# An attention-and-adapters kernel on one core: from a planned order of the engines to one written out as a table

## The chip, the cores and the metric

One core of one Trainium2 chip runs the kernel. The metric is the device time of one execution in microseconds; the median of several runs counts. The engines are PE (matmul), DVE (VectorE), ACT (ScalarE), POOL (GpSimd) and SP (SyncE, which here only issues DMAs). Each works off its own queue in the order in which the program issues instructions.

## The reference

Two stages follow each other. The first is a linear attention with a decaying state, for 4 batches, 8 heads, 768 steps and head size 48:

```
state = alpha[t, :, None] * state + outer(k[t], v[t])
y[t]  = q[t] @ state
```

The second takes y as x, 3072 rows of 384, through a mixture of 8 adapters of rank 16, of which each row uses the best 2:

```
logits = x @ w_gate                      # 384 -> 8
w = softmax over the best two logits
out = x + sum over those two e of w[e] * (x @ A[e]) @ B[e]
```

## The kernel before

The work is cut into 24 units: one batch and one chunk of 128 steps, all 8 heads at once. Units 0 to 11 are the chunks of batches 0 and 1 by turns, units 12 to 23 those of batches 2 and 3; unit u hands its state on to unit u + 2. For each unit:

- `ln` (ACT) takes logarithms of alpha, for two units in one instruction from unit 2 on; `cum` (PE) adds them up along the chunk; `exp` (ACT, two instructions) makes the decay factors for k and q.
- `kg` (POOL) multiplies k and q with them; it is called the product below. `vb` (POOL) casts v. `tr` (PE) transposes the product, `kq` (ACT) copies the transposes out of PSUM, `at` (PE) makes the scores, `msk` (DVE) masks them: the mask product.
- `st` (DVE) scales the state, `kv` (PE) adds to it, `av` (PE) makes the unit's output, `ysb` (ACT) copies it out: the output copy. `xb` (POOL, even units) casts it, `xt` (PE) transposes it, `xs` (ACT) copies that out.

Units are then taken together in gate groups: three units each, the last two groups being [21, 22] and [23]. For a group `z` (PE) makes x @ [A, w_gate]; `gm` is the maximum, `df` the difference to it, `ge` the choice of the best two, `gx` (ACT) the exponential, `wu` its product with the choice, `dn` the sum, `w` the reciprocal and the multiplication with it, `zw` the weighted x @ A (all DVE but `gx`). `zt` (PE) and `zs` (ACT) turn it, and for each unit `dl` (PE) multiplies with B and `o` (DVE) adds the result to the output; a store on SP follows.

What sets the order: a planner at the top of the file, `_plan`, `_arrivals`, `_ops` and `_order`. It knows a length for each instruction, an arrival time for each load and a priority for each kind of step, places all steps in time, and the program issues them in that order. Loads come in pieces of two units (384 KB) on two rings: SP issues those of k and q mostly, ACT those of alpha and v, ACT's standing among its other instructions. Loads of SP wait for the ACT instruction that was issued last before them, so that both rings keep pace:

```
    def pump(now):
        while loaded[0] < len(plan[0]):
            item = plan[0][loaded[0]]
            if arr["due", item] > now or not set(_readers(item)) <= did:
                return
            load_next(0)
```

A load is due 6 us ahead of the time at which the planner expects its transfer to begin. Each of alpha, k with q, and v has six buffers of two units. Stores begin when all loads have been issued. PSUM has two banks for the scores, two for the states, and four that all other results share (`SLOTS`, `M_t`). `KEEP` says how many buffers a step's result has: logarithms 2 (of two units each), `exp` 4, products 4, `am` 3.

Of the kernel before, what the change touches and what calls it, by code (L numbers as in the profile page):

```python
# [93 lines left out]
def _readers(item):

    _, x, u, n = item
    for p in range(u - 2 * NS, u - 2 * NS + n):
        if p >= 0 and x != "w":
            if x == "a":
                yield "ln", next(us[0] for us in LNS if p in us)  # L100
            else:
                yield dict(k="kg", q="kg", v="vb")[x], p


def _arrivals(plan):
    arr, now = {}, 2.6
    at = [0, 0]
    left = [0., 0.]

    def start(r):  # L110
        if at[r] < len(plan[r]):
            x = plan[r][at[r]]
            left[r] = (.1, .1, .02, .2)[x[2]] if x[1] == "w" else .197 * x[3]
            arr["due", x] = now - LEAD
        else:
            left[r] = None

    start(0), start(1)
    while left != [None, None]:
        rate = .205 if None in left else RATE / 2  # L120
        step = min(x / rate for x in left if x is not None)
        now += step
        for r in range(2):
            if left[r] is not None:
                left[r] -= step * rate
                if left[r] < 1e-9:
                    _, x, u, n = plan[r][at[r]]
                    for j in range(n):
                        arr[x, u + j] = now + .4
                    at[r] += 1  # L130
                    start(r)
    return arr


def _ops(arr):
    ops = {}

    def add(name, eng, length, deps, war=(), alloc=None, frees=None):
        ops[name] = (eng, length, list(deps), list(war), alloc, frees)

    gof = {u: g for g, us in enumerate(GROUPS) for u in us}
    lof = {u: us for us in LNS for u in us}
    prev = []
    for i, item in enumerate(_plan()[1]):
# [130 lines left out]
def kernel(  # L275
# [66 lines left out]
    def load_next(r):  # L342
# [10 lines left out]
        if r == 0:  # L353
            behind(dma)
# [331 lines left out]
```

## Time and profile before

| what | value |
|---|---|
| median of 3 runs | 105.65 us (105.19 to 106.39) |
| profiled execution | 105.82 us |
| its span, first to last instruction | 104.1 us |
| busy: PE, DVE, ACT, POOL | 73.4, 69.3, 66.9, 61.2 us |
| instructions of PE, DVE, ACT, POOL | 1088, 169, 152, 70 |
| read from and written to memory | 19.28 MB, 4.72 MB |

Busy time is the time in which an engine worked on an instruction; waiting and issuing DMAs do not count. The profile is of one execution, and its times are microseconds from the first instruction. A released wait is put down to what came last by the profile.

### The profile page before, as it was taken

Reading aid. Unit: us, or ns where it says so; the run is one execution under the profiler, and the core shown is the slowest. Engines: PE = TensorE matmul, PEld = TensorE weight load, DVE = VectorE, ACT = ScalarE, POOL = GpSimd, SP = SyncE. Lnnn points to the kernel's source line nnn. Section 1 sums busy time; section 2 is a strip of 40 time slices with the busy share of each in tenths; the row PEclk is TensorE's granted clock in tenths of the full one; section 3 lists DMA queues with packets and bytes.
Section 4 is the critical chain, followed back from the end, with each engine's and each line's share of the span. In section 5 each row is a group of like instructions: output and inputs, shape, how many; then the busy total and the mean of one; then the engine's idle time right before and its main releaser. Section 6 shows DMA issues by size and latency. Waiting matters only on the chain.

```text
span 104.1 us, 2882 instructions
## 1 busy us (share of the span) xinstructions
PE 73.4 (70%) x1088; PEld 55.9 (54%) x1088; DVE 69.3 (67%) x169; ACT 66.9 (64%) x152; POOL 61.2 (59%) x70
## 2 busy tenths in 40 slices
PE   0020668679796499299798799748998899985450
PEld 0010555458574477177586667546787777854110
DVE  4000035414746799997758898798889899988980
ACT  4024327967379578169897896957979994953200
POOL 5006551791972972964949969498395979610000
PEclk9999999999999999958999999999999999999955
DMA  2999999999999999969999999999999999306173
GB/s 42 258 259 260 260 261 242 259 259 219 254 254 218 259 209 247 264 133 259 254 222 260 252 250 251 260 260 227 233 253 258 346 375 361 131 0 227 42 269 145
DMA packets 103982, 24.18 MB, mean 232 GB/s; under 512 B 100768, under 2 KB 103968, under 8 KB 103968
## 3 DMA queue, kind: packets, MB, share of 16 engines
q1 hardware_dynamic: 54096, 14.36, 57.9%
q10 hardware_dynamic: 49872, 9.65, 45.6%
q8 instruction: 8, 0.13, 0.5%
q14 instruction: 6, 0.05, 0.1%
HBM read 19.28 MB, written 4.72 MB: 231 GB/s over the span
## 4 chain that ended last, share of the span: by engine, by line
PE 27%; DVE 26%; ACT 19%; issue 11%; POOL 7%; DMA 4%; ACTq 2%; SPq 0%; DVEq 0%
PE M_t L451 9%; DVE am L468 8%; POOL kgq L439 6%; ACT ex L329 4%; ACT kqt L332 4%; ACT lg L329 4%; DVE w L585 4%; DMA kq_t<-in_q_dram 4%; DVE o_t L627 4%; PE at_t L463 4%; PE M_t L612 3%; DVE zw L592 3%; ACT o_t L332 3%; DVE sb L475 3%; PE M_t L423 3%
## 5 line engine op out<-in xcount | busy, mean ns | idle before, releaser
L439 POOL TENSOR_TENSOR kgq<-kq_t,ex 128x768 bf16<-128x768 f32 x24 | 43.4, 1826 | 23.2 <-ACT ex L329 12.7
L468 DVE TENSOR_TENSOR am<-at_t,mask 128x1024 bf16<-128x1024 f32 x24 | 29.3, 1219 | 22.2 <-PE at_t L463 22.0
L329 ACT ACTIVATE ex<-M_t 128x392 f32<-128x392 f32 (+1 forms) x48 | 21.0, 514 | 2.0 <-PE M_t L427 1.7
L332 ACT COPY kqt<-M_t 128x512 f32<-128x512 f32 x24 | 14.2, 592 | 8.7 <-PE M_t L451 7.3
L451 PE MATMUL M_t<-ident,kgq 128*128 128x128 bf16 x192 | 17.2, 242 | 2.4 <-POOL kgq L439 1.2
L423 PE MATMUL M_t<-lg,suf 128*128 128x384 bf16 x24 | 8.9, 382 | 10.2 <-ACT lg L329 10.2
L451 PEld LDWEIGHTS <-kgq 128*128 128x128 bf16 x192 | 13.2, 108 | 5.0 <-POOL kgq L439 3.1
L329 ACT ACTIVATE lg<-a_t 128x768 bf16<-128x768 f32 (+1 forms) x13 | 10.4, 799 | 7.4 <-issue 5.8
L627 DVE TENSOR_TENSOR o_t<-M_t,o_t 128x384 f32<-128x384 f32 x24 | 12.6, 550 | 1.3 <-PE M_t L612 1.3
L475 DVE TENSOR_TENSOR sb<-S_t,ex 128x384 bf16<-128x384 f32 x20 | 11.0, 548 | 3.3 <-ACT ex L329 1.9
L332 ACT COPY o_t<-M_t 128x384 f32<-128x384 f32 x24 | 11.8, 495 | 2.1 <-PE M_t L506 2.0
L463 PE MATMUL at_t<-kqt 48*128 48x128 bf16 x192 | 10.4, 233 | 3.1 <-ACT kqt L332 2.5
L445 POOL CAST vb<-v_t 128x384 bf16<-128x384 f32 x24 | 11.5, 509 | 0.0
L506 PE MATMUL M_t<-vb,am 128*128 128x48 bf16 x192 | 9.2, 188 | 1.6 <-DVE am L468 1.4
L515 POOL CAST xb<-o_t 128x384 bf16<-128x384 f32 x12 | 6.1, 504 | 6.5 <-ACT o_t L332 4.2
L463 PEld LDWEIGHTS <-kqt 48*128 48x128 bf16 x192 | 6.0, 100 | 5.8 <-ACT kqt L332 3.8
L612 PE MATMUL M_t<-B_all,zs 128*128 128x384 bf16 x24 | 7.6, 374 | 2.0 <-ACT zs L332 1.2
L524 PE MATMUL M_t<-ident,o_t 128*128 128x128 f32 x36 | 7.4, 316 | 2.2 <-ACT o_t L332 1.9
L506 PEld LDWEIGHTS <-am 128*128 128x128 bf16 x192 | 7.3, 99 | 2.7 <-DVE am L468 2.5
L332 ACT CAST xs<-M_t 128x384 bf16<-128x384 f32 x12 | 5.9, 492 | 2.3 <-PE M_t L524 2.1
L543 PE MATMUL M_t<-W,xs 128*128 128x136 bf16 x72 | 5.8, 223 | 2.1 <-DVE W L391 1.0
L424 PEld LDWEIGHTS <-ident 128*128 128x128 bf16 x24 | 2.5, 103 | 8.6 <-issue 8.6
(48 smaller groups left out, 108.0 us busy)
## 6 DMA issues: line engine op xcount, KB each, us to landing
out_dram<-o_t SPq DMA_DIRECT2D x24, 192.0 KB, 3.0
kq_t<-in_k_dram SPq DMA_DIRECT2D x11, 384.0 KB, 6.1
a_t<-in_alpha_dram ACTq DMA_DIRECT2D x11, 384.0 KB, 5.8
kq_t<-in_q_dram SPq DMA_DIRECT2D x10, 384.0 KB, 5.6
v_t<-in_v_dram ACTq DMA_DIRECT2D x9, 384.0 KB, 5.3
v_t<-in_v_dram ACTq DMA_DIRECT2D x3, 192.0 KB, 4.2
v_t<-in_v_dram SPq DMA_DIRECT2D x3, 192.0 KB, 4.3
kq_t<-in_q_dram ACTq DMA_DIRECT2D x1, 384.0 KB, 4.0
```

The lines of the kernel that those rows point to most:

```text
L329: recent[:] = [nc.scalar.activation(*args, **kw)]
L332: recent[:] = [nc.scalar.copy(*args)]
L423: nc.tensor.matmul(r[:, 0:DM], suf[:, :], t[:, :, 0:D], start=True, stop=True)
L439: nc.gpsimd.tensor_tensor(out=kgq[u % KEEP["kg"]][:, :, :, 0:D], in0=kq_t[u // 2 % NS][:, :, u % 2, :, 0:D], in1=st["ex"][u][:, :, 0:DM].r ...
L445: nc.gpsimd.tensor_copy(out=st["vb"][u], in_=home("v", u)[:, u % 2, :, 0:D])
L451: nc.tensor.transpose(t[:, w, p, :], pair(kgq[u % KEEP["kg"]][:, w], p), ident[:, :])
L463: nc.tensor.matmul(at_t[:, hh, p, :], kq[rows, 0, p, :], kq[rows, 1, p, :], start=True, stop=True)
L468: nc.vector.tensor_tensor(out=st["am"][u].rearrange("p a b t -> p (a b) t"), in0=at_t.rearrange("p a b t -> p (a b) t"), in1=_bc_mid(mask[ ...
L475: nc.vector.tensor_tensor(out=st["sb"][u].rearrange("p a b d -> p (a b) d"), in0=S_t[u % 2].rearrange("p a b d -> p (a b) d"), in1=_bc(st[ ...
L506: nc.tensor.matmul(y[:, h * D:(h + 1) * D], st["am"][u][:, hh, p, :], st["vb"][u][:, h, :], start=(c == 0 and h == 0), stop=(h == H - 1), ...
L612: nc.tensor.matmul(bank("dl", u)[:, 0:DM], st["zs"][g][:, j * P:(j + 1) * P], B_all[:, :], start=True, stop=True)
L627: nc.vector.tensor_tensor(out=o_t[u], in0=bank("dl", u)[:, 0:DM], in1=o_t[u], op=ALU.add)
```

## The change

The planner goes. In its place stands a table of all steps in the order of issue, which the program reads word by word: `exp.7` is that step of unit 7 (or, for the gate, of that group), a last number is the PSUM bank, `Sk.8.2.xs1` is a load on SP's ring of k for two units from unit 8, held until the step xs of unit 1 on ACT is done, `Aa.8.2` a load of alpha on ACT's ring, `out.13` a store. The words ahead of the first step that is no load are issued first. Buffers that were taken from pools are now fixed rings, with 3 of each gate buffer rather than 2. The gate groups end with [18, 19], [20, 21], [22], [23]. For a group of one unit `ge` and `dn` go, `wu` is one instruction that compares, multiplies and adds up, `w` is the reciprocal alone, and `zw` multiplies with both factors. Unit 23's output stays in its PSUM bank, its delta is added to it there, and ACT copies the sum out (`HOLD`).

```diff
-GROUPS = [[0, 1, 2], [3, 4, 5], [6, 7, 8], [9, 10, 11], [12, 13, 14], [15, 16, 17],
-          [18, 19, 20], [21, 22], [23]]
+GROUPS = [[0, 1, 2], [3, 4, 5], [6, 7, 8], [9, 10, 11], [12, 13, 14], [15, 16, 17], [18, 19], [20, 21], [22],
+          [23]]
...
+HOLD = {23}
+KEEP = dict(lg=2, ex=4, kg=4, kt=4, am=3, sb=3, vb=4, xs=9, xb=3, mx=3, xe=3, wu=3, dn=3, w=3, zw=3, zs=3)
...
+ORDER = """
+Sa.1.1 Aa.0.1 Sk.0.1 Aa.2.2 Sv.2.2 ln.0 Aq.0.1 cum.0.0 Sk.1.1.ln0 Sv.0.1.ln0 exp.0 Av.1.1 ln.1 Aq.1.1 cum.1.1 exp.1
+vb.2 kg.0 Ak.2.2 Sq.2.2.exp1 Sw.2.0 ln.2 cum.2.2 tr.0.3 vb.0 kq.0 kg.1 Aa.4.2 at.0 Sv.4.2.kq0 kv.0 msk.0 exp.2
+cum.3.0 exp.3 vb.1 tr.1.1 kq.1 kg.2 Sk.4.2.exp3 Aa.6.2 at.1 Sq.6.2.kq1 av.0.3 msk.1 kv.1 ysb.0 kg.3 st.3 av.1.2
+tr.2.0 st.2 ysb.1 kq.2 vb.5 tr.3.1 ln.4 Sw.0.0 xb.0 Aq.4.2 vb.3 kq.3 cum.4.3 kv.2 vb.4 exp.4 at.2 kv.3 st.4 ln.6
+msk.2 Aw.1.0 cum.6.2 Sw.3.0 xt.1.0 Sk.6.2.ln6 Aa.10.2 at.3 av.2.1 msk.3 cum.5.3 xs.1 kg.4 ysb.2 Sk.8.2.xs1 av.3.0
+exp.5 Aa.8.2 st.5 xb.2 tr.4.1 ysb.3 kg.5 xt.0.3 cw.0 kq.4 Sq.8.2.ysb3 xs.0 at.4 exp.6 cum.7.0 xt.2.1 msk.4 xt.3.3
+ln.10 tr.5.2 xs.2 Av.6.2 exp.7 z.0.1 kg.6 kq.5 gm.0 av.4.0 xs.3 df.0 at.5 ln.8 msk.5 kg.7 tr.6.2 gx.0 Sq.10.2.ln8
+kv.4 kq.6 cum.8.3 Sv.8.2.gx0 ge.0 Ak.10.2 kv.5 wu.0 ysb.4 dn.0 av.5.2 w.0 xb.4 cum.9.0 ysb.5 zw.0 at.6 exp.8 vb.6
+st.6 zt.0.2 tr.7.1 vb.7 msk.6 zs.0 xt.4.3 exp.9 xt.5.2 kv.6 kg.8 Aa.12.2 st.7 xs.5 dl.0.0 xs.4 o.0 cum.10.2 kq.7
+dl.2.3 av.6.0 o.2 dl.1.1 kg.9 at.7 ysb.6 st.8 cum.11.3 exp.10 Sv.10.2.ysb6 o.1 tr.8.0 msk.7 Ak.12.2 exp.11 kg.10
+tr.9.1 kq.8 kv.7 kq.9 z.1.2 Sq.12.2.kq8 st.9 ln.12 Sk.14.2.kq8 at.8 gm.1 av.7.3 df.1 tr.10.0 ge.1 msk.8 vb.8 ysb.7
+gx.1 xb.6 Aa.14.2 kv.8 kq.10 Sa.16.2.gx1 vb.9 cum.13.1 wu.1 xt.7.3 dn.1 w.1 av.8.0 xs.7 zw.1 at.9 exp.13 cum.12.3
+st.10 xt.6.2 vb.10 msk.9 ysb.8 zt.1.1 xs.6 kv.9 xb.8 zs.1 Av.12.2 kg.11 exp.12 dl.5.0 dl.3.2 at.10 o.3 dl.4.1 xt.8.3
+o.5 av.9.2 xs.8 o.4 kg.12 tr.11.0 ysb.9 msk.10 z.2.3 kq.11 xt.9.1 Aq.14.2 ln.14 st.11 at.11 kg.13 gm.2 tr.12.2 xs.9
+df.2 cum.14.0 ge.2 msk.11 gx.2 kq.12 av.10.1 Sv.14.2.gx2 exp.14 vb.11 wu.2 at.12 ysb.10 dn.2 vb.13 w.2 tr.13.2
+Ak.16.2 xb.10 zw.2 av.11.0 kq.13 vb.12 cum.15.1 msk.12 ysb.11 zt.2.3 xt.10.2 zs.2 kg.14 xt.11.0 exp.15 dl.8.3 kv.12
+at.13 o.8 xs.11 Sq.16.2.exp15 dl.6.1 msk.13 xs.10 av.12.3 Aa.18.2 ln.16 kg.15 z.3.0 tr.14.2 o.6 ysb.12 gm.3 cum.16.1
+kq.14 av.13.3 df.3 st.14 xb.12 gx.3 exp.16 at.14 ge.3 vb.15 tr.15.2 wu.3 dn.3 Av.16.2 vb.14 msk.14 kv.13
+Sa.20.2.exp16 ysb.13 cum.17.1 kq.15 kv.14 xt.12.3 exp.17 w.3 Sk.18.2.kq15 at.15 st.15 kg.16 av.14.2 ln.18 zw.3 kv.15
+msk.15 xt.13.1 ysb.14 dl.7.0 Aq.18.2 Sv.18.2.ysb14 xs.12 xb.14 tr.16.2 xs.13 o.7 kg.17 zt.3.3 st.16 xt.14.1 kq.16
+cum.18.0 st.17 xs.14 at.16 zs.3 av.15.2 exp.18 msk.16 Sq.20.2.zs3 z.4.1 vb.16 ysb.15 vb.17 tr.17.3 Ak.20.2 gm.4
+dl.11.0 kv.16 kq.17 df.4 ge.4 o.11 dl.10.2 gx.4 kv.17 ln.20 wu.4 o.10 cum.19.3 kg.18 av.16.0 dn.4 exp.19
+Sa.22.2.ln20 w.4 xt.15.2 st.18 Sq.22.2.ln20 at.17 ysb.16 zw.4 cum.20.3 xs.15 Sk.22.2.ysb16 msk.17 kg.19 exp.20
+zt.4.0 tr.18.1 cum.21.2 zs.4 kq.18 dl.9.3 st.19 av.17.0 o.9 dl.13.1 Sv.22.1.kq18 vb.19 ysb.17 at.18 o.13 exp.21
+dl.12.3 xb.16 tr.19.0 msk.18 vb.18 xt.16.1 Av.20.2 kq.19 dl.14.2 Sv.23.1.exp21 kg.20 kv.19 xs.16 out.13 o.12 xt.17.0
+out.2 at.19 o.14 xs.17 av.18.1 msk.19 z.5.3 kg.21 ysb.18 out.1 ln.22 kv.18 gm.5 tr.20.2 ge.5 av.19.0 df.5 st.20 gx.5
+kq.20 xb.18 tr.21.1 wu.5 st.21 ysb.19 at.20 dn.5 kq.21 vb.20 w.5 xt.18.2 xt.19.0 msk.20 vb.21 xs.18 out.0 cum.22.1
+xs.19 cum.23.2 exp.22 z.6.0 zw.5 at.21 exp.23 gm.6 zt.5.3 msk.21 av.20.1 kg.22 out.11 zs.5 kv.21 ysb.20 dl.17.2
+dl.16.3 out.10 df.6 ge.6 av.21.1 o.17 gx.6 out.6 kv.20 wu.6 ysb.21 o.16 xb.20 out.4 tr.22.2 dn.6 kg.23 st.22 dl.15.1
+xt.21.3 kq.22 w.6 o.15 xs.21 at.22 zw.6 xt.20.2 out.12 msk.22 xs.20 zt.6.1 vb.22 tr.23.3 out.14 zs.6 z.7.0 out.15
+kq.23 dl.18.2 st.23 av.22.1 out.9 gm.7 at.23 o.18 ysb.22 out.7 dl.19.3 df.7 xb.22 msk.23 out.3 gx.7 vb.23 xt.22.1
+out.17 xs.22 ge.7 out.18 av.23.2 wu.7 o.19 z.8.1 out.16 ysb.23 dn.7 gm.8 w.7 out.19 xt.23.3 df.8 zw.7 gx.8 out.5
+wu.8 xs.23 zt.7.0 w.8 out.8 zs.7 z.9.3 zw.8 dl.20.0 gm.9 zt.8.1 df.9 o.20 gx.9 zs.8 dl.21.1 wu.9 out.20 dl.22.0 w.9
+zw.9 o.22 zt.9.3 o.21 zs.9 out.22 dl.23 out.21 o.23 out.23
+"""
...
-def _plan():
-def _arrivals(plan):
-def _ops(arr):
-def _order(arr):
...
+    def load(ring, x, u, n, *name):
+        eng = dict(S=nc.sync, A=nc.scalar)[ring]
...
+        if name:
+            behind(dma, name[0])
...
     def wu(g):
         n = len(GROUPS[g])
+        if n == 1:
+            nc.vector.scalar_tensor_tensor(
+                out=wut[g % KEEP["wu"]][:, 0, :], in0=zv(g)[:, 0, E * R:NZ], scalar=mx[g % KEEP["mx"]][:, 0, 1:2],
+                in1=xe[g % KEEP["xe"]][:, 0, :], op0=ALU.is_ge, op1=ALU.mult, accum_out=dnt[g % KEEP["dn"]][:, 0:1])
+            return
...
     def w(g):
...
+        if n == 1:
+            return
...
     def zw(g):
...
+        if n == 1:
+            nc.vector.scalar_tensor_tensor(
+                out=zo, in0=z3[:, 0], scalar=dnt[g % KEEP["dn"]][:, 0:1], in1=_bc(wut[g % KEEP["wu"]][:, 0, :], R),
+                op0=ALU.mult, op1=ALU.mult)
...
     def dl(u):
         g, j = gof[u]
+        hold = u in HOLD
+        nc.tensor.matmul(bank("av" if hold else "dl", u)[:, 0:DM], zst[g % KEEP["zs"]].bitcast(F2)[:, j * P:(j + 1) * P],
+                         B_all[:, :], start=not hold, stop=True, skip_group_check=True)
...
     def o(u):
+        if u in HOLD:
+            act_copy(o_t[u], bank("av", u)[:, 0:DM])
+        else:
+            nc.vector.tensor_tensor(out=o_t[u], in0=bank("dl", u)[:, 0:DM], in1=o_t[u], op=ALU.add)
...
     with tc.manual_schedule():
+        for name, i, *more in todo:
+            i = int(i)
+            if name in RUN:
+                slot[name, i] = int(more[0]) if more else None
+                RUN[name](i)
...
+            else:
+                load(*name, i, int(more[0]), *more[1:])
```

## Rows read from the trace of the kernel before

**Rows 1.** Page, part 1: busy time, share of the span and instructions.

```profile
PE 73.4 (70%) x1088; PEld 55.9 (54%) x1088; DVE 69.3 (67%) x169; ACT 66.9 (64%) x152; POOL 61.2 (59%) x70
```

**Rows 2.** Page, parts 2 and 3: memory traffic in 40 equal slices, and totals.

```profile
GB/s 42 258 259 260 260 261 242 259 259 219 254 254 218 259 209 247 264 133 259 254 222 260 252 250 251 260 260 227 233 253 258 346 375 361 131 0 227 42 269 145
...
HBM read 19.28 MB, written 4.72 MB: 231 GB/s over the span
```

**Rows 3.** The tile v_t, from 78.7 to 79.3: the last load.

```profile
L351 SPq DMA_DIRECT2D v_t<-in_v_dram x1: 368/368/368, 78.9 to 78.9; - x1
...
DMA to landing us min/median/max: 3.4/3.4/3.4
```

**Rows 4.** Stretches: length, then busy (xinstructions) by engine, PE clock, DMA share, GB/s.

```profile
14.65:26.76 12.11, 10.26 (x116) 7.72 (x115) 5.34 (x7) 8.73 (x18) 6.21 (x6) 1.00 1.19 246
26.76:41.00 14.24, 11.01 (x183) 8.67 (x183) 10.71 (x29) 9.92 (x23) 8.96 (x11) 1.00 1.18 239
41.00:91.09 50.09, 42.80 (x713) 33.79 (x710) 42.91 (x88) 40.31 (x93) 39.51 (x41) 0.97 1.13 255
91.09:104.10 13.01, 6.18 (x54) 3.33 (x51) 9.23 (x38) 3.27 (x11) 0.50 (x1) 0.79 0.37 137
```

**Rows 5.** Timeline from 7 to 23: start, length, instruction [idle before, what ended it].

```profile
8.10 0.48 ACT L329 ACTIVATE ex<-M_t 128x384 f32<-128x384 f32 x1
...
8.67 1.81 POOL L439 TENSOR_TENSOR kgq<-kq_t,ex 128x768 bf16<-128x768 f32 x1 [6.43 <-DMA kq_t<-in_q_dram]
...
11.14 2.10 ACTq L351 DMA_DIRECT2D a_t<-in_alpha_dram  x1
...
13.28 0.59 ACT L332 COPY kqt<-M_t 128x512 f32<-128x512 f32 x1 [1.27 <-PE S_t L489]
...
14.65 1.23 DVE L468 TENSOR_TENSOR am<-at_t,mask 128x1024 bf16<-128x1024 f32 x1 [12.56 <-PE at_t L463]
...
16.36 0.84 ACT L329 ACTIVATE lg<-a_t 128x768 bf16<-128x768 f32 x1 [0.24 <-ACT kqt L332]
...
18.84 3.58 POOL L439 TENSOR_TENSOR kgq<-kq_t,ex 128x768 bf16<-128x768 f32 x2 [0.70 <-ACT ex L329]
```

**Rows 6.** Waits: who waited for whom, in total, how often, the longest.

```profile
POOL kgq L439 <- ACT ex L329: 12.7, 9, 2.6
```

**Rows 7.** Timeline of the end: the last product, last mask product and last gate.

```profile
86.58 1.83 POOL L439 TENSOR_TENSOR kgq<-kq_t,ex 128x768 bf16<-128x768 f32 x1
...
91.09 1.21 DVE L468 TENSOR_TENSOR am<-at_t,mask 128x1024 bf16<-128x1024 f32 x1
...
93.43 0.47 ACT L332 COPY o_t<-M_t 128x384 f32<-128x384 f32 x1
...
94.92 0.48 ACT L332 CAST xs<-M_t 128x384 bf16<-128x384 f32 x1 [1.01 <-PE M_t L524]
...
97.69 0.15 DVE L578 TENSOR_REDUCE dn<-wu 128x1 f32<-128x8 f32 x1
...
98.27 0.17 DVE L585 TENSOR_TENSOR w<-wu,dn 128x8 f32<-128x8 f32 x1
...
98.82 0.28 DVE L592 TENSOR_TENSOR zw<-M_t,w 128x128 bf16<-128x128 f32 x1
...
100.68 0.56 DVE L627 TENSOR_TENSOR o_t<-M_t,o_t 128x384 f32<-128x384 f32 x1 [0.18 <-PE M_t L612]
```

**Rows 8.** The tile w (ns: least, median, most), and the timeline around one.

```profile
L585 DVE TENSOR_TENSOR w<-wu,dn x9: 168/233/1590, 36.7 to 98.3; 128x24 f32<-128x24 f32 x7, 128x16 f32<-128x16 f32 x1, 128x8 f32<-128x8 f32 x1
...
40.93 3.58 POOL L439 TENSOR_TENSOR kgq<-kq_t,ex 128x768 bf16<-128x768 f32 x2 [2.61 <-ACT ex L329]
...
41.19 1.59 DVE L585 TENSOR_TENSOR w<-wu,dn 128x24 f32<-128x24 f32 x1
```

**Rows 9.** Page, part 6: issues of one load, KB each, median us to landing.

```profile
kq_t<-in_q_dram SPq DMA_DIRECT2D x10, 384.0 KB, 5.6
```

More of the change, by code (lines that the diff above doesn't have):

```diff
@@ L94, in _readers @@
[L94 to L102, printed above, removed]
-def _arrivals(plan):
[L106 to L132, printed above, removed]
@@ L352, in load_next @@
             out=dst, in_=SRC[x][b:b + n, :, c * C:(c + 1) * C, :].rearrange("b h j d -> j (b h) d"))
-        if r == 0:
-            behind(dma)
-    for i in range(FIRST):
-        load_next(i % 2)
+        if name:
+            behind(dma, name[0])
+    todo = [t.split(".") for t in ORDER.split()]
+    while todo[0][0][0] in "SA":
+        (ring_, x), u, n = todo.pop(0)
+        load(ring_, x, int(u), int(n))
     suf = consts.tile([P, P], F2, name="suf")
@@ L384 @@
     nc.vector.tensor_copy(out=ident4, in_=ident)
+    ring = lambda name, shape, dt: [consts.tile(shape, dt, name=f"{name}{i}") for i in range(KEEP[name])]
+    ex = ring("ex", [P, 2, DM + 2 * NP], F4)
+    kt = ring("kt", [P, 512], F4)
+    am = ring("am", [P, 2, NP, P], F2)
+    sb = ring("sb", [P, NP, 2, D], F2)
+    vbt = ring("vb", [P, H, D], F2)
+    xst = ring("xs", [P, NF, P], F2)
+    xbt = ring("xb", [P, DM], F2)
+    mx = ring("mx", [P, 3, 8], F4)
+    xe = ring("xe", [P, 3, E], F4)
+    wut = ring("wu", [P, 3, E], F4)
+    dnt = ring("dn", [P, 3], F4)
+    wt = ring("w", [P, 3, E], F4)
+    zwt = ring("zw", [P, 3, E, R], F2)
+    zst = ring("zs", [P, 3 * HP], F4)
     W = consts.tile([P, NF, NZ], F2, name="W")
@@ L506, in av @@
                 nc.tensor.matmul(
[L507 to L508 removed]
+                    y[:, h * D:(h + 1) * D], am[u % KEEP["am"]][:, hh, p, :], vbt[u % KEEP["vb"]][:, h, :],
+                    start=(c == 0 and h == 0), stop=(h == H - 1 and u not in HOLD), skip_group_check=True)
     def ysb(u):
@@ L638, in store, with cw @@
         t0 = b * S + c * C
-        dma = nc.sync.dma_start(out=out[t0:t0 + C, :], in_=o_t[u])
-        if not stored:
-            behind(dma)
-        stored.append(u)
-    with tc.manual_schedule():
-        for s, i in order:
-            if (s, i) == ("z", 0):
-                cast_weights()
-            RUN[s](i)
-            did.add((s, i))
-            pump(when[s, i][0])
-            if s == "o":
-                done.append(i)
-            if loaded == [len(plan[0]), len(plan[1])]:
-                while done:
-                    store(done.pop(0))
+        nc.sync.dma_start(out=out[t0:t0 + C, :], in_=o_t[u])
+    def cw(_):
+        cast_weights()
+    RUN = dict(ln=ln, cum=cum, exp=exp, kg=kg, vb=vb, tr=tr, kq=kq, at=at, msk=msk, st=stf, kv=kv,
+               av=av, ysb=ysb, xb=xb, xt=xt, xs=xs, z=z, gm=gm, df=df, ge=ge, gx=gx, wu=wu, dn=dn,
+               w=w, zw=zw, zt=zt, zs=zs, dl=dl, o=o, out=store, cw=cw)
+    with tc.manual_schedule():
+        for name, i, *more in todo:
[3 more added lines that the diff above has]
+                RUN[name](i)
+                if recent:
+                    acts[f"{name}{i}"] = recent.pop()
+            else:
+                load(*name, i, int(more[0]), *more[1:])
 _INS = ['q', 'k', 'v', 'alpha', 'moe_w_gate', 'moe_A', 'moe_B']
```

285 lines of the change are left out of this document (41 added, 244 removed).

## The prediction

> **What bounds the kernel now.** I read the share of each engine first: none is busy for more than 70% of the span [rows 1], so the bound has to be looked for stage by stage. Next come the slices of the memory traffic and the landing of the last load. Loads run at 258 to 261 GB/s in the best slices and with dips to 219, 209 and 133 between them [rows 2]; the last load is issued at 78.9 us and lands 3.4 us later, at 82.3 [rows 3]. The 19.28 MB read [rows 2] would need 74.4 us at 259 GB/s; begun at about 2.4 they would be in at about 77. So the dips cost some 5 us, and yet the span goes on for 21.8 us after the last load: an engine is behind. The table of stretches tells which. VectorE (DVE) is busy for 5.34 of 12.11 us, then 10.71 of 14.24, 42.91 of 50.09 and 9.23 of 13.01 [rows 4]. ScalarE is nearly as full (40.31) in the long stretch, GpSimd a little less (39.51); all three stand close to what the loads allow. I cut at two places of DVE: the start of the first mask product, 14.65 [rows 5], and the start of the last, that of unit 23, 91.09 [rows 7]. The span is then 14.65 (head) + 58.96 (DVE busy between the two, the first three stretches) + 17.48 (DVE idle between: 6.77, 3.53 and 7.18) + 13.01 (all behind 91.09) = 104.10. The profiled execution took 105.82, so 1.72 lies outside the span, and it stands 0.17 above the median of 105.65.
>
> **Head.** In the row of the first product of unit 0 GpSimd is said to have waited for a load of q [rows 5], but the exponential it also needs ended at 8.58, just before it began: that was the last to come. In the table q of unit 0 is fourth in its ring, behind alpha of unit 0 and two units of alpha, and each ring gets half of 259 GB/s, 1.52 us for one unit's 0.197 MB: it lands at 2.4 + 4 x 1.52 = 8.5. The exponential no longer decides, the load does, and with the cast ahead of it the product starts at about 9.0 rather than 8.67. The gain comes after it: the copy of unit 0's transposes waited until 13.28, because ScalarE's own DMA issue held its queue from 11.14 to 13.24 [rows 5]. In the table the load that will be held in this way (k of units 2, 3) stands ahead of that copy and of logarithm 2, and is through at about 10. Product 9.0 + 1.81, transposes about 1.4, copy 0.59, scores and a start: the first mask product at about 13.6, 1.05 earlier. Bounds: 12.8 (the copy as soon as the product) and 15.2 (ScalarE held for 2.1 us once more).
>
> **Logarithms further ahead.** Logarithm 2 ran at 16.36 behind the copy of unit 1, and so product 2 at 18.84 [rows 5], though its loads had been in for some time. GpSimd's products waited for exponentials 9 times, 12.7 us [rows 6]. In the table logarithm 2 stands ahead of the first copy, 6 ahead of exponential 5, 10 ahead of 8. The instructions are the same 13 and 48, so they cost nothing new; what is gained is that a product starts when k and q land. DVE gets little of it early: mask product 2 needs the copy of unit 2, which the table puts behind two output copies of units 0 and 1, so it comes at about 23.5. I take the idle of the first two stretches as it was plus the 1.05 by which DVE starts early: 6.77 + 3.53 + 1.05 = 11.35. From 41 us on the lead in products (I follow the table to product 6 at about 31, and mask product 10 at about 49) lets DVE find work; of 7.18 idle I keep a quarter, 1.8. Ends: 0, and the 7.18 of before.
>
> **DVE's order.** Ahead of the last mask product there are now 19 additions and not 15, the whole gate of units 18 and 19, and two small steps of the gate of 20 and 21. An addition is 0.56 alone [rows 7] and some 0.50 in a row; four make 2.0, the gate pieces 1.3 to 2.0. So 3.3 to 4.0 of the 9.23 us that were busy behind that point are moved ahead; I take 3.6: 58.96 + 3.6 = 62.56.
>
> The multiplication w is the one with a strange price: least 168 ns, most 1590 [rows 8]. The longest began at 41.19 and ended at 42.78; a product on GpSimd began at 40.93, and at its mean (3.58 for two, 1.81 each up to where the next starts) ended at 42.74. All of w's excess is about 3.8 us. Seven of them stand ahead of the last mask product instead of six; I leave their total as it was, with ends at -3.8 (none meets a product) and at 7 x 1.41 - 3.8 = +6.1 (each meets the start of one). The Trainium skill, "SBUF - State Buffer", section "SBUF: two separate sides", says why this speaks against the change: a DVE instruction with two SBUF inputs is blocked by a GpSimd instruction that reads SBUF, for all of it. The row agrees (1590 ns), and by that rule a GpSimd that is kept busier makes w dearer; the last rival has it.
>
> **Behind the last mask product: groups of 2, 2, 1, 1, and the sum in PSUM.** Four pieces, before against after. Mask product to the end of the copy xs: 91.09 to 95.40 [rows 7], 4.31; in the table the exponential of the gate of 22 stands ahead of xs, so some waiting stays, 3.9. From there to the end of zw: 95.40 to 99.10, 3.70, in which DVE works off two gates by turns. For one unit ge, the sum dn (0.15) and the multiplication w (0.17) go [rows 7], and the other gate of one unit is through before; maximum, difference, exponential, one addition, two fused steps and a reciprocal: 2.15. No row shows the fused form with its running sum: it costs between one small step (0.15) and two (0.32), the fused zw between 0.28 and 0.28 + 0.17; I take 0.18 and 0.30, near the single steps, since they work on as many elements. The Trainium skill, "VectorE: DVE Perf Modes", section "Two Vector instructions with no wait between them", counts an instruction that also writes its accumulator as two; no run here shows it, and by that rule my estimate would be 0.15 later. From zw to the end of the last sum: 99.10 to 101.24, 2.14; now with a copy on ScalarE (0.47 in its row of 93.43 [rows 7]) for an addition of 0.56, 2.0. The store and the end: 2.86, the same. Together 13.01 becomes 10.9, less 2.1. The bank that holds unit 23's output until its delta is added isn't asked for by anything else in the table.
>
> **Loads and stores that move.** The last load in the table (v of units 20, 21) stands behind exponential 21, and the cast of unit 20 stands ahead of product 22 on GpSimd. Behind mask product 17 that is: output copy and exponential 1.4, landing 4.2, two casts 1.0, product 1.83, cast 0.5, product 1.83, and 2.68 to mask product 23 (88.41 to 91.09 [rows 7]): 13.4. DVE has about 16 us of work in its order between the same two points, so this hides with 2.6 to spare; from 2.6 on it costs in full. The 24 stores, in a new order on SP, take some 0.5 us each, 12 us from about 78 on; the last few are made after 94, so they hide with about 4 to spare.
>
> **Sum.** 13.6 + 62.56 + 11.35 + 1.8 + 10.9 = 100.2 of span; + 1.72 = 101.9; - 0.17 = **101.7 us** for the median.
>
> **Rivals.** *Saturated.* The loads flow without dips and DVE never waits after 41 us (-1.8) while half of w's excess goes (-1.9): 98.0 to 99.7, say 98.3. For it: the dips of rows 2. Against it: ScalarE has 40.31 busy of 50.09 and is asked for by every unit. Its floor is the last load at 77, casts, two products, 2.68, 10.9: about 97.
>
> *No gain.* DVE's idle time after 41 us stays at 4.7 to 6.8, for the work put ahead of the last mask product costs more than the end saves: 104.6 to 106.7, say 105.5. For it: two buffers of logarithms and four of exponentials are unchanged, so that "further ahead" ends at two pairs. Against it: the additions put forward fill just such holes.
>
> *Loads on a short leash (slower).* In the table loads are issued nearer to their use: q of 18 behind the output copy of 14, k of 20 behind that of 15, q of 16 behind exponential 15, where before q of 18 stood behind the xs copy of 11. One such loop is landing 5.6 [rows 9], product 1.83, 2.68 to the mask product, 1.21, and 1.6 to the end of the output copy at 93.90 [rows 7]: 12.9 us for 4 to 6 units, say 4.5. About 16 units are left at 41 us, 3.6 loops, 46.4; my forecast has 48.3 for them, so the loop is just hidden. If each loop queues for 1.6 more, the gain is gone; at 2.4 more it is 3.6 x 15.3 = 55.1, last mask product at 96.1, and **108.5 us**. For it: waits of 1.4 for one exponential (12.7 / 9) are what such a loop collects. Against it: just these waits are to go.
>
> *w behind products.* Each of the seven meets the start of a product: +6.1, 107.8.
>
> **How the numbers follow.** Forecast (99.7 to 104.6) 0.55, saturated 0.17, no gain 0.14, short leash 0.10, w 0.04. One per cent, 1.06 us, is about what a measurement can tell here, with three runs 1.2 apart: faster is below 104.6, 0.72; same 0.14; slower, over 106.7, 0.14. The range leaves out the lower half of the saturated case and the slower cases: 98.3 to 106.2.
>
> **What would show it.** Right: the last load lands at 77 to 79; logarithm 2 ends before 11; products wait for exponentials less than 5 us in all; DVE's busy time between its first and last mask product is 62 to 63 and its idle time 12 to 15; the last mask product starts near 89, the end of the span less than 11.2 behind it. Wrong: dips in the slices of 40 to 70 us with idle rings (leash); w rows above 1 us in most groups; the last product held by a cast of v; or first mask product after 15.

## The result and the profile after

The changed kernel takes 98.97 us (median, 98.55 to 99.22) where the kernel before took 105.8 in the same runs: a ratio of 0.9351 [0.9287, 0.9415], 6.8 us less. The forecast of 101.7 named the direction, and its range held the time, but it was 2.7 too high. The profiled execution took 98.55; its span is 96.8, and 1.75 lies outside. Of the kernels below, those with late logarithms and with logarithm 2 late were profiled in executions 1.5 and 1.6 us slower than their medians, so only large differences are read from these two traces.

The page of the changed kernel: its first part (busy time), then the memory traffic in 40 slices and the totals.

```profile
PE 70.8 (73%) x1088; PEld 54.9 (57%) x1088; DVE 67.9 (70%) x171; ACT 67.4 (70%) x155; POOL 61.2 (63%) x70
...
GB/s 34 248 260 259 260 260 258 260 250 254 285 262 259 254 234 259 259 259 252 250 232 257 260 263 256 257 256 207 260 223 236 258 170 400 262 392 335 225 202 123
...
HBM read 19.28 MB, written 4.72 MB: 248 GB/s over the span
```

Against [rows 1, 2] the engines' busy times differ by at most 2.6 us; about the same work is done in 7.3 us less of span. The dip to 133 is gone. Up to 77 us the lowest slice behind the start is now 207.

The table of stretches, cut at the first and the last mask product as in [rows 4] (length, then busy and count by engine, PE clock, DMA share, GB/s); the last row is a stretch of DVE alone.

```profile
13.31:26.76 13.45, 9.79 (x138) 7.40 (x137) 6.85 (x8) 8.06 (x16) 8.45 (x10) 1.00 1.26 261
26.76:41.00 14.24, 13.15 (x204) 10.84 (x201) 11.83 (x24) 12.71 (x30) 11.82 (x10) 0.88 1.25 254
41.00:86.52 45.52, 40.28 (x687) 32.14 (x684) 42.17 (x106) 37.52 (x89) 34.38 (x37) 1.00 1.16 259
86.52:96.80 10.28, 4.08 (x33) 2.06 (x32) 6.03 (x24) 3.00 (x10) 0.96 (x2) 0.80 0.63 233
...
69.00:86.52 17.52, 17.30 (x43) 1.00 1.05 272
```

Read as in the prediction, the third engine column is DVE's. The span is 13.31 (head) + 60.85 (DVE busy) + 12.36 (DVE idle: 6.60, 2.41, 3.35) + 10.28 (behind the last mask product) = 96.80. Against before: head -1.34, busy +1.89, idle -5.12, end -2.73; together -7.30. Most of the gain is DVE's idle time, and the second part is the end.

Who waits for whom (total, times, longest):

```profile
POOL vb L266 <- DMA v_t<-in_v_dram: 9.5, 5, 6.3
POOL kgq L261 <- DMA kq_t<-in_q_dram: 6.2, 2, 4.2
...
POOL kgq L261 <- ACT ex L138: 2.7, 2, 1.9
...
DVE am L289 <- PE at_t L285: 15.1, 4, 11.2
```

The products' wait for exponentials fell from 12.7 us in 9 places [rows 6] to 2.7 in 2. What they wait for most now is data: q, twice. The chain that ended last (start, length) shows the same from the other end. It passes through loads, and product 16 begins at 60.73 as q of 16, issued at 54.56, lands at 60.57:

```profile
19.03 5.50 DMA kq_t<-in_q_dram
24.65 1.83 POOL kgq L261
...
54.56 6.01 DMA kq_t<-in_q_dram
60.73 1.82 POOL kgq L261
```

The timeline (start, length, instruction, idle before and what ended it): the start, the cast of the weights, exponential 15, and the end.

```profile
8.86 0.84 ACT L138 ACTIVATE lg<-a_t 128x768 bf16<-128x768 f32 x1
...
11.94 0.59 ACT L141 COPY kt<-M_t 128x512 f32<-128x512 f32 x1 [2.24 <-PE M_t L272]
...
13.31 1.22 DVE L289 TENSOR_TENSOR am<-at_t,mask 128x1024 bf16<-128x1024 f32 x1 [11.22 <-PE at_t L285]
...
15.07 1.81 POOL L261 TENSOR_TENSOR kgq<-kq_t,ex 128x768 bf16<-128x768 f32 x1 [0.82 <-ACT ex L138]
...
22.00 1.22 DVE L289 TENSOR_TENSOR am<-at_t,mask 128x1024 bf16<-128x1024 f32 x1
...
26.86 1.82 POOL L261 TENSOR_TENSOR kgq<-kq_t,ex 128x768 bf16<-128x768 f32 x1
...
27.14 1.76 DVE L212 CAST W<-W_st 128x384 bf16<-128x384 f32 x1 [1.29 <-DMA W_st<-in_moe_A_dram]
...
53.59 0.91 ACT L138 ACTIVATE ex<-M_t 128x392 f32<-128x392 f32 x2
...
86.52 1.21 DVE L289 TENSOR_TENSOR am<-at_t,mask 128x1024 bf16<-128x1024 f32 x1
...
89.38 0.48 ACT L141 CAST xs<-M_t 128x384 bf16<-128x384 f32 x1
...
91.53 0.22 DVE L388 SCALAR_TENSOR_TENSOR wu<-M_t,mx,xe 128x8 f32<-128x8 f32 x1
91.67 0.08 DVE L388 DVE_READ_ACCUMULATOR wu<-M_t,mx,xe 128x1 f32 x1
91.79 0.16 DVE L402 RECIPROCAL dn<-dn 128x1 f32<-128x1 f32 x1
91.99 0.35 DVE L413 SCALAR_TENSOR_TENSOR zw<-M_t,dn,wu 128x128 bf16<-128x128 f32 x1
...
93.57 0.48 ACT L141 COPY o_t<-M_t 128x384 f32<-128x384 f32 x1 [0.65 <-PE M_t L434]
```

Logarithm 2 now ends at 9.70 instead of 17.20, and product 2 starts at 15.07 instead of 18.84 [rows 5]. The copy of unit 0's transposes comes at 11.94 instead of 13.28, for no issue of a load holds ScalarE's queue in front of it. The last load (tile v_t, its issue):

```profile
L157 SPq DMA_DIRECT2D v_t<-in_v_dram x1: 1730/1730/1730, 76.4 to 76.4; - x1
...
DMA to landing us min/median/max: 4.1/4.1/4.1
```

It lands at 80.4, 1.9 earlier than before [rows 3].

### The profile page after: what moved, and what is told of

Same layout as the page of the kernel before. It is cut to its first block, busy times and chain, and to the rows that moved or that the text cites. A ratio compares the mean times of both kernels' runs of the same rounds, so it can differ in the third digit from the quotient of the medians.

```text
span 96.8 us, 2861 instructions
## 1 busy us (share of the span) xinstructions
PE 70.8 (73%) x1088; PEld 54.9 (57%) x1088; DVE 67.9 (70%) x171; ACT 67.4 (70%) x155; POOL 61.2 (63%) x70
## 4 chain that ended last, share of the span: by engine, by line
PE 25%; DVE 23%; ACT 16%; DMA 15%; POOL 11%; issue 5%; ACTq 1%; POOLq 0%; DVEq 0%
DMA kq_t<-in_q_dram 12%; POOL kgq L261 11%; DVE am L289 7%; PE M_t L272 6%; DVE o_t L441 6%; ACT ex L138 5%; ACT kt L141 4%; PE at_t L285 4%; DMA a_t<-in_alpha_dram 4%; DVE w L405 2%; ACT o_t L141 2%; PE M_t L343 2%; PE M_t L246 2%; PE M_t L361 2%; PE M_t L434 2%
## 5 line engine op out<-in xcount | busy, mean ns | idle before, releaser
L272 PE MATMUL M_t<-ident,kgq 128*128 128x128 bf16 x192 | 16.7, 238 | 3.6 <-POOL kgq L261 3.6
L141 ACT COPY kt<-M_t 128x512 f32<-128x512 f32 x24 | 14.1, 594 | 7.4 <-PE M_t L272 7.1
L141 ACT COPY o_t<-M_t 128x384 f32<-128x384 f32 x25 | 12.3, 491 | 4.9 <-PE M_t L326 4.1
L285 PE MATMUL at_t<-kt 48*128 48x128 bf16 x192 | 10.2, 229 | 2.5 <-ACT kt L141 2.1
L285 PEld LDWEIGHTS <-kt 48*128 48x128 bf16 x192 | 5.9, 98 | 5.5 <-ACT kt L141 3.7
L141 ACT COPY xs<-M_t 128x384 bf16<-128x384 bf16 x12 | 5.9, 495 | 1.6 <-PE M_t L343 1.6
```

Of the source, the lines that this page charges most:

```text
L141: recent[:] = [nc.scalar.copy(*args)]
L272: nc.tensor.transpose(t[:, w, p, :], pair(kgq[u % KEEP["kg"]][:, w], p), ident[:, :])
L285: nc.tensor.matmul(at_t[:, hh, p, :], kq[rows, 0, p, :], kq[rows, 1, p, :], start=True, stop=True)
```

## The experiments

The theory was that of the prediction: logarithms that run ahead let products start when data lands, DVE's holes fill, and the end is shorter. The rivals were that the load order alone, or the end alone, brings the gain, and that DVE's own work sets the pace. Twelve kernels ran; each ratio is to the kernel before. The order of engines and that of loads were separated by building the table from the planner's orders.

**The program, with the order of before.** The changed program with before's order and loads as its table, gate groups of before, nothing fused, nothing held.

```diff
-HOLD = {23}
+HOLD = set()
-ln.0 Aq.0.1 cum.0.0 Sk.1.1.ln0 Sv.0.1.ln0 exp.0 Av.1.1 ln.1 ...
+ln.0 cum.0.0 exp.0 Av.2.2 Sq.2.2.exp0 ln.1 kg.0 cum.1.1 exp.1 ...
```

> The changed program, but its table holds the order, the loads, the gate groups (2 and 1 at the end, unfused) and the last addition of the kernel before; what is left of the change is the fixed rings with three gate buffers. Both theories: 105.8, within 1 (104.8 to 106.8), span cut as before (last mask product near 91, 13 behind it). Under 104.8 would mean that the rings do part of it.

106.23 us, 1.0004 [0.996, 1.0047]; head, busy, idle, end 14.77, 58.87, 17.65, 13.04, as both theories had it. The rewritten program (fixed rings, three gate buffers) costs and brings nothing by itself. The whole difference is in the table and the end.

**The new end alone.** The planner's order, made anew for groups of 2, 2, 1, 1, with the fused steps and the sum in PSUM.

```diff
-GROUPS = [..., [18, 19, 20], [21, 22], [23]]
+GROUPS = [..., [18, 19], [20, 21], [22], [23]]
+HOLD = {23}
```

> The order and loads of the planner of before, planned with gate groups 2, 2, 1, 1, the fused single-unit gate and unit 23's sum in PSUM. If the end's parts add up as the traces say (13.01 to 10.28 behind the last mask product), 103.1 (102.5 to 104). If the gates put ahead cost DVE as much as they save at the end, 105 to 106.

109.12 us, 1.03 [1.0233, 1.0366]: slower, and above both forecasts. The stretches of this kernel, up to and behind the last mask product:

```profile
14.77:91.01 76.24, 64.24 (x1005) 50.21 (x1003) 58.71 (x121) 59.34 (x133) 54.68 (x56) 0.98 1.15 251
91.01:107.33 16.32, 7.72 (x54) 3.90 (x51) 9.82 (x40) 4.08 (x14) 0.50 (x1) 0.66 0.29 109
```

Ahead of the last mask product nothing moves. Behind it are 16.32 us and not 13.01, for the planner puts four groups there where three were, each with its own run through PE, ACT and DVE, and the last group's maximum comes 10.2 us behind the last mask product (101.23) instead of 4.8 (95.89). In this order more and smaller groups make the end longer; the table puts [18, 19] ahead of the last mask product.

**The two halves of the table.** First the table's engine order with before's loads, then the planner's engine order with the table's loads (both with the new end).

```diff
 # engines of the table, loads of before
-Sa.1.1 Aa.0.1 Sk.0.1 Aa.2.2 Sv.2.2 ln.0 Aq.0.1 ...
+Sa.0.1 Ak.0.1 Sq.0.1 Aa.1.1 Sk.1.1 Av.0.1 Sv.1.1 Aq.1.1 Aa.2.2 Sk.2.2 ln.0 ...
 # engines of the planner, loads of the table
-Av.1.1 ln.1 Aq.1.1 cum.1.1 exp.1 vb.2 kg.0 Ak.2.2 Sq.2.2.exp1 ...
+Av.1.1 ln.1 Aq.1.1 kg.0 cum.1.1 exp.1 Sq.2.2.exp1 Sw.2.0 Ak.2.2 vb.0 ...
```

> The engines' order of the table with the load order of before, each load behind the same ScalarE step as there, or next to it where a buffer or a reader asks for it. Theory 1, that products now start when their loads land and VectorE idles less because of the engines' order: 98.5 to 100.5. Rival, that the load table (what is loaded when, on which ring) gives the gain: 103 to 106, with products waiting for loads for over 10 us more than in the changed kernel.

118.53 us, 1.1193 [1.1117, 1.1268], far above both forecasts. Waits of GpSimd in this kernel:

```profile
POOL vb L275 <- DMA v_t<-in_v_dram: 14.6, 2, 12.8
POOL xb L343 <- ACT o_t L150: 11.5, 5, 4.9
```

The first entry of GpSimd's queue in the table is the cast of v of unit 2. With the old loads that v lands late; GpSimd stands for 12.8 us, product 0 begins at 15.5 and not at 9.0, and the first mask product at 19.79. That explains 6.5 of the 19.6 us over the changed kernel. The rest is DVE idle, 24.40 instead of 12.36, beside waits of the same kind. A table with that one cast moved was not run, so it is not shown that the old loads can't serve any form of the new order.

> The planner's order of the engines (with the gate groups 2, 2, 1, 1 and the sum in PSUM as in the run of the tail alone) with the load table of the change. Theory 1: within 1.5 of the run of the tail alone, 102 to 105. Rival (load table): 99 to 101.

127.31 us, 1.1986 [1.1884, 1.2088], the slowest of all and again above both forecasts. The memory traffic in its 40 slices, and how long SP's loads waited for logarithms, here and in the changed kernel (total, times, longest):

```profile
GB/s 72 260 259 260 258 258 114 249 119 0 71 255 260 202 213 256 169 241 260 238 43 116 225 84 170 185 259 238 193 100 235 224 287 395 306 94 127 228 84 62
```

```profile
SPq L165 <- ACT lg L146: 20.9, 4, 8.8
```

```profile
SPq L157 <- ACT lg L138: 5.1, 2, 3.0
```

The holds of the loads name steps of ScalarE. Where those run late, loads do too: slices of 0, 43, 71 and 84. That is the prediction's short leash. As these two kernels were built, neither half has a gain of its own that could be added to the other's. Each is fitted to its partner.

**The holds alone.** The table without them; loads of SP wait for their buffers only.

```diff
-Sk.1.1.ln0 Sv.0.1.ln0 exp.0 ... Sq.2.2.exp1
+Sk.1.1 Sv.0.1 exp.0 ... Sq.2.2
```

> The changed kernel with its loads in the same order on both rings, but SP's are held by nothing except free buffers. If the holds only cost time (dips in the loads): 97 to 98.5. If they keep both rings in step, so that what is needed first lands first: SP's ring runs ahead, alpha on ScalarE's ring comes late, logarithms wait for it more than 5 us longer in all, and the time is 100 to 106.

111.38 us, 1.0486 [1.0395, 1.0578], above the 100 to 106 of the second forecast. The traffic of this kernel, and ScalarE's waits:

```profile
GB/s 38 259 260 259 261 242 249 259 280 167 260 259 253 252 242 257 259 254 213 209 258 260 266 252 260 251 250 232 50 135 1 254 387 228 7 189 314 216 175 119
```

```profile
ACT o_t L150 <- DMA kq_t<-in_q_dram: 3.1, 1, 3.1
ACT ex L147 <- DMA G_st<-in_moe_w_gate_dram: 3.0, 1, 3.0
ACT kt L150 <- DMA W_st<-in_moe_A_dram: 2.6, 1, 2.6
```

The wait that this forecast named did not come: logarithms wait for alpha 2.3 us, in the changed kernel 2.2 (there the only load that ScalarE waits for). Here ScalarE's own DMA issues stand still until a load of the other ring has landed: an issue of alpha starts at 15.15, as the load of the gate's weights lands (issued at 9.36, 5.8 us), and the exponentials of unit 2 behind it come at 15.57 instead of 12.42. SP runs ahead with loads that nobody needs yet. At the end it is the other way: SP has issued its last load at 70.3, and ScalarE's are still to come, at 73.7, 78.0 and 83.7, one by one: slices of 50, 135 and 1. The last load lands at 87.4. So the holds are part of the gain.

**Logarithms late.** Logarithms, sums and exponentials of units 6 to 21 as late as in the order of before. Holds that named one of them now name the step ahead, and PSUM banks are dealt out anew.

```diff
-... kv.3 st.4 ln.6 msk.2 Aw.1.0 cum.6.2 ... at.4 exp.6 cum.7.0 ... exp.7 z.0.1 kg.6 kq.5 ...
+... kv.3 st.4 msk.2 Aw.1.0 ... kq.5 ln.6 cum.7.1 cum.6.2 exp.6 kg.6 exp.7 ...
```

> The changed kernel, but for units 6 to 21 logarithm, sum and exponentials stand as late against the copy of the transposes as in the order of before (exponentials of a pair behind the copy of the unit ahead of it); loads that were held by a moved step are held by the step ahead of it. Theory 1: products wait for exponentials again, 5 us or more in total, and the time is 101 to 104. Rival, that the place of the logarithms matters little beside the loads: within 0.6 of 99.0.

112.61 us, 1.0618 [1.0528, 1.0708]. That is above both forecasts. Its waits of GpSimd, and its traffic:

```profile
POOL kgq L270 <- ACT ex L147: 18.5, 7, 4.9
```

```profile
GB/s 43 259 260 259 260 258 260 238 255 284 260 260 121 248 243 17 237 180 164 247 163 151 208 64 224 178 260 260 259 189 233 249 315 362 159 63 351 288 94 189
```

The products' wait for exponentials is back, larger than before the change (18.5 against 12.7), and DVE is idle for 25.5 us. So logarithms ahead take that wait away, as the forecast had it. What this is worth in time is not shown: 13.6 us is more than the whole gain, and the loads held behind late steps come late too (slices of 121, 17 and 64).

**Logarithm 2 alone.** The first step of it: logarithm 2 and the sums of units 2 and 3 behind the copy of unit 1, as before.

```diff
-Sw.2.0 ln.2 cum.2.2 tr.0.3 vb.0 kq.0 ... msk.0 exp.2 cum.3.0 exp.3 vb.1 tr.1.1 kq.1 kg.2
+Sw.2.0 tr.0.3 vb.0 kq.0 ... msk.0 vb.1 tr.1.1 kq.1 ln.2 cum.2.2 exp.2 cum.3.0 exp.3 kg.2
```

> The changed kernel, but logarithm, sums and exponentials of units 2 and 3 stand behind the copy of unit 1, as in the kernel before. Forecast: products 2 and 3 come some 3.5 us later but mask product 2 waits for other things: +0 to +0.8 (99.0 to 99.8). Rival: loads of k and q that hang on exponential 3 come later too, and the lead is never made up: +2 to +3.5.

100.93 us, 0.9522 [0.9456, 0.9588], 2.0 slower than the changed kernel, the lower end of the rival's range. Product 2 starts at 17.99 and not at 15.07, and the second, third and fourth mask product come 1.8 to 2.5 later. Time lost there is not won back: the pieces of the start are on the path.

**DVE's work.** Two kernels take work from DVE ahead of the last mask product. One leaves the product wu in PSUM, so that w has a single operand in SBUF:

```diff
-out=wut[g % KEEP["wu"]][:, 0:n, :], in0=scratch(g, 1),
+out=scratch(g, 1), in0=scratch(g, 1),
```

> The changed kernel, but the product of choice and exponential is left in the PSUM bank of its gate, so that the multiplication w reads one operand from PSUM and not two from SBUF. If w waits because it and GpSimd's product both read SBUF, w is 0.17 to 0.22 in all groups (in the profile of after 1.8 us of excess in all) and the kernel gains 0.5 to 1.6 where VectorE is the bound; if VectorE is not the bound, w gets short and the time stays. Rival, that w waits for something else: w keeps rows near 1 us.

98.72 us, 0.9317 [0.9268, 0.9367]. The tile w (ns: least, median, most) in the changed kernel, and then in this one:

```profile
L405 DVE TENSOR_TENSOR w<-wu,dn x8: 174/183/1107, 34.4 to 88.8; 128x24 f32<-128x24 f32 x6, 128x16 f32<-128x16 f32 x2
```

```profile
L405 DVE TENSOR_TENSOR w<-M_t,dn x8: 175/182/184, 34.1 to 89.1; 128x24 f32<-128x24 f32 x6, 128x16 f32<-128x16 f32 x2
```

The long ones are gone: the second SBUF operand was the cause. (One w, at 83.64, still lies within a product of GpSimd, 82.66 to 84.49, and takes 0.17.) DVE's busy time fell by 1.22 (60.85 to 59.63), its idle time rose by 1.46, and the time can't be told from that of the changed kernel.

The other moves the additions of units 15 to 18, with their deltas, behind the last mask product and ahead of `wu` of the next gate; PSUM banks are dealt out anew from the second gate on.

```diff
-... kv.21 ysb.20 dl.17.2 dl.16.3 out.10 df.6 ge.6 av.21.1 o.17 gx.6 ... o.16 ... o.15 ... o.18 ...
+... msk.23 ... ge.7 av.23.1 dl.15.3 o.15 out.15 dl.16.3 o.16 dl.17.3 o.17 out.17 dl.18.3 o.18 out.18 wu.7 ...
```

> The changed kernel with the additions of units 15 to 18, and their products with B, moved behind the last mask product (4 x 0.5 us of VectorE). The forecast had it that work ahead of the last mask product costs VectorE its time there: then the last mask product comes 2 us earlier, the end is 2 us longer, 98.6 to 99.5. Rival: ahead of it this work fills time in which VectorE would wait for products anyway, so moving it back costs: the last mask product stays within 0.6 of 86.5 and the time is 100.4 to 101.2.

103.08 us, 0.9735 [0.9678, 0.9792], the rival's mechanism, but more than its 100.4 to 101.2. Its stretches up to and behind the last mask product:

```profile
13.46:86.62 73.16, 64.39 (x1018) 51.29 (x1016) 59.31 (x134) 57.80 (x135) 54.89 (x55) 0.98 1.20 261
86.62:101.42 14.80, 6.78 (x37) 2.85 (x36) 8.26 (x28) 2.98 (x11) 0.96 (x2) 0.65 0.40 149
```

The last mask product starts at 86.62, in the changed kernel at 86.52. DVE has 1.54 less to do ahead of it and is idle for 1.49 more. So the four additions ahead cost nothing: they lie in holes. Behind it they cost 4.5 us, more than their 2.2, for in this kernel the four deltas share one PSUM bank and come 1.0 to 1.2 apart. Both kernels say the same: although DVE works for 17.30 of the 17.52 us up to the last mask product, its amount of work isn't what sets it.

**The pieces of the end.** Within the table: groups of 2, 2, 2 (its last steps rearranged for that); separate steps for groups of one; the sum of unit 23 on DVE.

```diff
 # groups of 2, 2, 2
-GROUPS = [..., [18, 19], [20, 21], [22], [23]]
+GROUPS = [..., [18, 19], [20, 21], [22, 23]]
 # separate steps
-df.8 zw.7 gx.8 out.5 wu.8 xs.23
+df.8 ge.8 zw.7 gx.8 out.5 wu.8 dn.8 xs.23
-        if n == 1:
+        if n == 0:
 # no sum in PSUM
-HOLD = {23}
+HOLD = set()
```

> The changed kernel with gate groups [18, 19], [20, 21], [22, 23]: the last two units in one gate of two (unfused), at the place of unit 23's. The last chain gets longer by a product of x (0.15), a wider zw (0.1), the sum and the multiplication (0.4), while VectorE has one gate less at the end. Theory 1: +0.3 to +1.0. Rival, that fewer gates at the end are worth more than a short last one: -0.3 to -0.8.

100.85 us, 0.9504 [0.9454, 0.9553], 1.9 more than the changed kernel by the medians and above the forecast. By the two profiled executions it is 1.1, all of it at the end: 11.36 us behind the last mask product and not 10.28.

```profile
86.56:97.92 11.36, 3.47 (x33) 1.91 (x32) 5.91 (x21) 2.78 (x8) 0.96 (x2) 0.83 0.54 199
```

> The changed kernel, but the two gates of one unit with the separate choice, sum and multiplication of the others: three more VectorE instructions for each, two of them on the last chain. By the trace of after, from wu to zw 0.81 in the fused form against about 1.08: theory 1, +0.3 to +0.9. Rival, that the end is held by ScalarE and PE between the gates: no change.

100.31 us, 0.9462 [0.9412, 0.9511], 1.3 more, above the forecast. From the start of wu to the end of zw of the last group: 1.08 us, fused 0.81; the end is 10.78, 0.5 more, as forecast. The rest lies ahead of the edit: the last mask product started at 87.48, 0.96 later, and product 4 stood at 25.09 instead of 24.65 already, ahead of every step that differs. No row shows why, so a difference of under 1 us between two of these kernels says little by itself.

> The changed kernel, but unit 23's delta is added by VectorE as for the others (its product with B in the bank that the output has left). The end is 0.48 for ScalarE's copy against 0.56 for the addition: theory 1, +0.1 (98.9 to 99.3), not to be told from no change. Rival, that the sum in PSUM takes VectorE out of a queue at the end (two additions of units 21 and 22 stand ahead of it there): +0.4 to +0.6.

99.32 us, 0.9374 [0.9331, 0.9417]: not told from the changed kernel. The addition that comes back takes 0.56 (from 94.14), the copy in its place 0.48.

## Why the prediction was right, and where it was off

The mechanism held: the gain comes from idle time of DVE and from the end. Of span it named 100.2; 96.8 came. By its terms:

**Head**, 13.6: measured 13.31. Both reasons are in the rows. Product 0 began at 9.0 as forecast, with q of unit 0 landed at 8.8, and the copy at 11.94 no longer stood behind a load.

**Idle time**, 11.35 + 1.8 = 13.15: measured 12.36, but split otherwise. The early part was put too high (6.60 + 2.41 = 9.01): mask product 2 came at 22.00, not at 23.5, and the next at 23.91, where it had been 26.76 [rows 4], so much of the lead of logarithm 2 reached DVE early. The run with logarithm 2 late agrees: there they come 2.3 and 2.5 later. The late part was put too low (3.35 against 1.8).

**DVE's busy time**, 62.56: measured 60.85, the term that was off most. DVE by line between its first and last mask product (busy, mean ns), before and then after:

```profile
L627 DVE TENSOR_TENSOR o_t<-M_t,o_t 128x384 f32<-128x384 f32 x15 | 7.9, 551 | 1.1 <-PE M_t L612 1.1
L585 DVE TENSOR_TENSOR w<-wu,dn 128x24 f32<-128x24 f32 x6 | 4.8, 806 | 0.2
...
L389 DVE CAST W<-W_st 128x384 bf16<-128x384 f32 x1 | 0.3, 348 | 0.0
```

```profile
L441 DVE TENSOR_TENSOR o_t<-M_t,o_t 128x384 f32<-128x384 f32 x19 | 10.1, 546 | 1.2 <-PE M_t L434 1.2
...
L405 DVE TENSOR_TENSOR w<-wu,dn 128x24 f32<-128x24 f32 (+1 forms) x7 | 3.0, 431 | 0.2
...
L212 DVE CAST W<-W_st 128x384 bf16<-128x384 f32 x1 | 1.8, 1764 | 1.3 <-DMA W_st<-in_moe_A_dram 1.3
```

Four more additions took 2.2, priced at 2.0. The total of w was left as it was and fell by 1.8, its excess over 0.18 each from some 3.8 to 1.8; the cast of W took 1.4 of that back. Together the rows rose by 3.5, close to the 3.6 of the sum. But where instructions follow each other closely their rows overlap, and the time covered rose by 1.89 only: that is nearly all of the miss. The deeper fault is that the sum charged moved work as if DVE were the bound; the two kernels of DVE's work show that taking it away mainly returns idle time.

**End**, 10.9: measured 10.28. Up to the end of xs 3.35 (forecast 3.9), to the end of zw 2.47 (2.15), to the end of the last sum 1.71 (2.0), store 2.75 (2.86). The fused step with its running sum was put at 0.18; its two rows take 0.22 and 0.08 and the reciprocal starts 0.26 behind it; zw took 0.35 and not 0.30. Against groups of 2, 2, 2 the split of the last pair is worth about 1.1 and the fused steps about 0.5, by their stretches. What share of the 2.7 gained is theirs no run shows, for the last group of before was [23] alone too.

**Of the Trainium skill's rules**, that of "SBUF — State Buffer", section "SBUF: two separate sides", is borne out here: with one SBUF operand fewer, no w is longer than 184 ns, where 1107 was seen. It did not speak against this change in the end, for GpSimd's products and w met less often. That of "VectorE: DVE Perf Modes", section "Two Vector instructions with no wait between them", agrees too: the accumulator's read stands as a row of its own, 0.08 us, not the 0.15 estimated.

**The rivals.** The time, 98.97, lies just below the forecast's own 99.7 to 104.6 and inside the saturated case (98.0 to 99.7). Two of its three conditions came true, loads with few dips and half of w's excess gone; the third didn't, DVE idle for 3.35 after 41 us, and the early idle time (9.01 for 11.35), the head and the end made up for it. No gain and w behind products fell. The short leash is in no slice of the changed kernel (lowest from 40 to 70 us: 207), but it holds one product. q of 16, which that rival named, is issued at 54.56, just behind exponential 15 (54.50), and product 16 waited some 2.1 us for it. Memory ran at 256 to 263 GB/s meanwhile, so the rings were not idle. The kernel with late logarithms and the one with the planner's order show what a longer leash costs.

**The signs.** Right: logarithm 2 (9.70), waits for exponentials (2.7), idle (12.36), the end (10.28). Missed: busy time, and the last load, 80.4 where 77 to 79 was named. The prediction took v of units 20 and 21 for it; that was issued at 71.49 and landed at 76.4, but v of unit 23 (`Sv.23.1.exp21`) stands behind it in the table. Slices of 207, 223, 236 and 170 remain ahead of 80.4. The last mask product, put near 89, came at 86.52.

What sets the 26 us up to the last mask product stays open, and half of the lead is lost there. Mask product 15 starts 9.5 us earlier than before, the last one 4.6 [rows 7]. Mask product 15 before, and then mask product 15 and product 22 in the changed kernel:

```profile
69.81 1.21 DVE L468 TENSOR_TENSOR am<-at_t,mask 128x1024 bf16<-128x1024 f32 x1
```

```profile
60.32 1.21 DVE L289 TENSOR_TENSOR am<-at_t,mask 128x1024 bf16<-128x1024 f32 x1
...
79.44 1.83 POOL L261 TENSOR_TENSOR kgq<-kq_t,ex 128x768 bf16<-128x768 f32 x1 [1.92 <-ACT ex L138]
```

In the changed kernel and five close variants the last mask product comes 25.5 to 25.9 behind the start of product 16, and that start (60.7 to 61.6) stands, in the changed kernel, right behind the landing of its load. Product 22 then waits 1.92 for its exponentials, most of the 2.7 that is left of that wait. No run tells which of ScalarE, PE and GpSimd holds that stretch; less work on DVE shortens it by 0.3 at most (25.5 with the short w, 25.8 with the additions late, 25.8 in the changed kernel).

## What to carry to other kernels

An order of engines and an order of loads are one design: test them together, since each alone can be worse than what was there (here +12% and +20%). Before charging moved work to an engine, ask whether it lands in the engine's holes; a busy share of 99% over a stretch doesn't prove that its work sets the time, and a kernel with some of that work taken out does tell. Run the small early steps that release everything else as far ahead as their buffers allow, and look for which queue entry, a DMA issue too, stands in front of them.

## What the runs showed of the hardware

- A DVE cast of 384 elements from SBUF to SBUF took 348 ns before and 1764 in the changed kernel, where it began at 27.14 under a GpSimd product of 26.86 to 28.68. It has one SBUF input, so the two-input rule of the Trainium skill ("SBUF — State Buffer", section "SBUF: two separate sides") doesn't cover it; whether it ran in one of the two-port modes that this section names beside that rule, no row shows.
- A DVE instruction with a running sum has a second row, DVE_READ_ACCUMULATOR, of 0.08 us, that partly overlaps the first.
- DMA issues on ScalarE's queue waited for landings of loads that SP had issued (in the kernel without holds 2.6 to 3.1 us each, three times, and 1.8 once), and so did the computing instructions behind them. What ties the two rings together, no row shows.
